# Earlier weight loads, another order in the opening, moved steps in the middle and later square roots in a fused attention and MLP kernel

## The chip, the cores and the metric

The kernel runs on one core of one Trainium2 chip. Times are device microseconds of one execution. A kernel was run once, with a profile, and where a few per cent matter in several timed rounds as well, beside runs of the kernel before on the same chip. All times compared below are of runs in the fast state. "Span" is the profiled execution from the first to the last instruction; it is some 1.7 us shorter than the time.

## The reference, cut to what matters

```python
def _attn_ref(q, k, v, lam):          # 4 batches, 8 heads, 768 rows, head size 64
    for b in range(nb):               # blocks of rows, a state of 64 x 64 per head
        intra = einsum('bhic,bhjc->bhij', qb, kb) * Dmask    # decay inside the block
        intra = einsum('bhij,bhjd->bhid', intra, vb)
        inter = einsum('bhid,bhde->bhie', qb * lam_pow, kv_state)
        out[:, :, sl] = intra + inter
        kv_state = lam_block * kv_state + einsum('bhsd,bhse->bhde', kb * rev_pow, vb)

def _moe_ref(x, g_ln, w_ch1, w_ch2):  # x: 4 x 768 x 512 out of the attention
    mu, var = mean(x), mean((x - mu) ** 2)
    xn = (x - mu) / sqrt(var + 1e-06) * g_ln
    return x + maximum(xn @ w_ch1, 0.0) @ w_ch2        # 512 -> 2048 -> 512
```

## The kernel before: the parts that matter

The work is cut into 12 units of 256 rows (a "window" is a unit's keys, queries and values). A unit goes through casts, transposes, scores and masks, products with values and state, and a norm; then its 256 rows are one group of the MLP. The two MLP weights come in four pieces each, with a cast from fp32 to bf16 in the transfer, issued by GpSimd. SyncE issues nearly everything else. A piece is held back by `behind`, a tiny GpSimd copy (0.19 us in the traces) that reads something and so waits for its landing: 7.24 us for the first piece in the kernel before.

```python
def load_w1(c):
    nc.gpsimd.dma_start(w1[c], moe_w_ch1[...])            # 512 KB in SBUF
def load_window(u, after_pool=False, parts=1):            # keys, queries, values of unit u
    got = {name: inp.tile([128, H, 2 * D], F32, tag=name + "in", ...) for name in "kqv"}
    if after_pool:
        nc.gpsimd.memset(got["k"][:, 0, 0:1], 0.0)        # the load waits for GpSimd's place
    ...  nc.sync.dma_start(got[name][:, hs, :], source(...))
def behind(tile_ap):
    seen_p = wk.tile([128, 1], F32, tag="seen_p", name="seen_p")
    nc.gpsimd.tensor_copy(seen_p, tile_ap)

# constants: allocated one after another, ahead of all the working buffers
lam_v = const.tile([128, H, 2], F32)
lam_c = const.tile([128, H], F32)
lam_s = const.tile([128, NP], F32)

# opening ...
open_window(0); load_window(1)
in_k(0, nc.vector, HA)                    # cast of the first half of the keys
transpose_pe(0, 0, (0, 1))
nc.scalar.activation(lam_c, lnlam, ACT.Exp, scale=float(C))
in_q(0, nc.vector, HA)
in_k(0, nc.gpsimd, HB)                    # second half of the keys
load_w1(0)                                # first weight piece, behind that cast
...
norm(0, 0, early=True)
behind(w1[0][:, 0, 0:1])                  # ... the next waits for the first
load_w1(1); in_q(1, nc.gpsimd); load_w1(2); load_w1(3); in_v(1, nc.gpsimd); load_w2(0)
behind(w1[2][:, 0, 0:1])
load_window(2, after_pool=True)
# ...
def p4(u):                                # at the end of a unit's norm
    to_xT(u, 0); to_xT(u, 1)              # transposed input of the MLP, by DMA from unit 2 on
    rstd_of(u)                            # ScalarE: square root of the variance
# ... and a plan: after MLP step n of TensorE, these attention steps
add(29, (s4, 3), (p4, 3), (transpose_dma, 4))
add(41, (s1, 4))
```

## Time and profile before

230.24 us, median of 3 runs (229.79 to 230.64); the span of the profiled run is 228.9 us at a granted TensorE clock of 1.000.

| engine | busy us | share of the span |
|---|---|---|
| TensorE matmuls | 204.7 | 89% |
| TensorE weight loads (beside the matmuls) | 139.4 | 61% |
| VectorE | 101.4 | 44% |
| ScalarE | 84.9 | 37% |
| GpSimd | 73.4 | 32% |

The table of stages of the kernel before shows where TensorE loses time after its first 15 us. Each row is a stretch in us from the span's start, its length, then busy us and instructions of each engine; the last two numbers are the mean busy share of the DMA engines and GB/s.

```profile
core 0: us, PE busy (x) PEld busy (x) DVE busy (x) ACT busy (x) POOL busy (x), PEclk, DMA share, GB/s
15.00:20.00 5.00, 2.80 (x30) 2.48 (x31) 1.78 (x4) 1.62 (x3) 1.82 (x3) 1.00 0.57 130
20.00:60.00 40.00, 35.18 (x538) 24.00 (x536) 17.55 (x37) 18.30 (x32) 20.83 (x27) 1.00 1.12 218
60.00:120.00 60.00, 56.82 (x986) 38.27 (x984) 30.45 (x63) 20.29 (x37) 27.46 (x32) 1.00 1.11 235
120.00:210.00 90.00, 89.27 (x1243) 59.13 (x1241) 40.57 (x87) 33.26 (x63) 17.45 (x20) 1.00 0.61 106
```

From 20 to 120 us TensorE loses 8.0 us of 100 while the DMA share is above 1 (it sums the times of packets, so a share above 1 means that some packets overlap on an engine). From 120 us on it loses 0.73 of 90, and the DMA share is 0.61. One more row of the page will be needed: what SyncE's queue moved in the whole run (packets, MB, the time of its packets as a share of 16 engines' span).

```profile
q1 hardware_dynamic: 71008, 32.65, 68.7%
```

The busy time in that row is 0.687 x 228.9 = 157.3 us of all 16 engines. I call it the queue's engine time below.

### The profile page before, as it was taken

The page shows a single profiled execution, that of the slowest core. Times are in us where ns is not written, and L with a number is a line of the kernel's source. Part 1 is how long each engine was busy: PE and PEld are TensorE (multiplying, and loading weights), DVE is VectorE, ACT ScalarE, POOL GpSimd, SP SyncE. Part 2 cuts the span into 40 slices and gives each one's busy share as a digit, 9 for nine tenths or more (in the row PEclk, how much of TensorE's full clock was granted, in tenths as well). Part 3 has the DMA queues.
Part 4 walks back from the last instruction along what each step waited for, and adds up shares of the span by engine and source line. Part 5 has one row for each costly group of instructions (what it writes and reads, how often), then busy time and mean ns, then how long its engine had stood idle before and what let it go on. Part 6 is the DMA issues. An engine that isn't in the chain of part 4 may idle for free.

```text
span 228.9 us, 6911 instructions
## 1 busy us (share of the span) xinstructions
PE 204.7 (89%) x3056; PEld 139.4 (61%) x3056; DVE 101.4 (44%) x216; ACT 84.9 (37%) x154; POOL 73.4 (32%) x93
## 2 busy tenths in 40 slices
PE   0647697989999999698999999999999999999992
PEld 0537586644575675285486485585684784765862
DVE  2761552428256155833554535437338237152011
ACT  4625557511153243035135145154252351350610
POOL 3608415707745064668028045063010010000000
PEclk9999999999999999999999999999999999999999
DMA  5996999999999999999999699695193212311303
GB/s 140 284 250 101 191 247 218 144 281 273 190 297 267 160 259 262 159 262 239 183 273 177 126 218 175 142 216 72 42 141 74 51 47 46 95 26 23 93 3 92
DMA packets 75566, 37.42 MB, mean 163 GB/s; under 512 B 31248, under 2 KB 72464, under 8 KB 75536
## 3 DMA queue, kind: packets, MB, share of 16 engines
q1 hardware_dynamic: 71008, 32.65, 68.7%
q0 software_dynamic: 4224, 4.19, 11.8%
q8 instruction: 24, 0.39, 0.7%
q10 hardware_dynamic: 304, 0.14, 0.2%
q14 instruction: 6, 0.05, 0.1%
HBM read 27.53 MB, written 6.29 MB: 148 GB/s over the span
## 4 chain that ended last, share of the span: by engine, by line
PE 52%; DMA 24%; POOL 8%; issue 6%; DVE 5%; ACT 2%; SPq 1%; DVEq 0%; POOLq 0%
PE pm L360 24%; PE pm L398 22%; DMA w<-in_moe_w_ch_dram 7%; DMA qin<-in_q_dram 6%; DMA kin<-in_k_dram 6%; POOL kq L171 3%; DMA xT<-xc 2%; DMA kqT<-kq 2%; DVE stats L310 2%; POOL kq L163 2%; POOL vb L176 2%; PE po L273 2%; PE pm2h L389 2%; DVE xc L312 1%; PE pk L232 1%
## 5 line engine op out<-in xcount | busy, mean ns | idle before, releaser
L360 PE MATMUL pm<-xT,w 128*128 128x256 bf16 x736 | 87.3, 273 | 3.4 <-DMA xT<-xc 1.3
L363 ACT ACTIVATE hT<-pm 128x512 bf16<-128x512 f32 x92 | 54.6, 596 | 91.7 <-PE pm L360 91.6
L398 PE MATMUL pm<-w,hT 128*128 128x512 bf16 x368 | 83.0, 379 | 0.4
L360 PEld LDWEIGHTS <-w 128*128 128x128 bf16 x736 | 69.8, 98 | 15.7 <-issue 3.0
L398 PEld LDWEIGHTS <-hT 128*128 128x128 bf16 x368 | 34.9, 98 | 41.6 <-ACT hT L363 2.6
L238 POOL TENSOR_TENSOR Sn<-Stmp,lam_s 128x256 bf16<-128x256 f32 x16 | 9.8, 613 | 77.2 <-DVE Stmp L242 77.2
L218 DVE TENSOR_TENSOR mA<-sc,keep 128x512 bf16<-128x512 f32 x44 | 28.6, 682 | 12.7 <-PE sc L208 12.6
L414 DVE SCALAR_TENSOR_TENSOR o<-pm,rstd,x 128x512 f32<-128x512 f32 x23 | 17.1, 745 | 35.4 <-PE pm L398 35.2
L310 DVE BATCH_NORM_STATS2 stats<-x 128x6 f32<-128x512 f32 x20 | 13.8, 689 | 28.2 <-ACT x L308 28.2
L171 POOL TENSOR_TENSOR kq<-qin,lam_q 128x512 bf16<-128x512 f32 x22 | 22.6, 1048 | 10.4 <-DMA qin<-in_q_dram 10.2
L176 POOL TENSOR_TENSOR vb<-vin,lam_v 128x1024 bf16<-128x1024 f32 (+1 forms) x13 | 23.0, 1774 | 2.7 <-DMA vin<-in_v_dram 2.6
L312 DVE SCALAR_TENSOR_TENSOR xc<-po,mv,g_row 128x512 bf16<-128x512 f32 x24 | 18.0, 751 | 2.0
L242 DVE TENSOR_TENSOR Stmp<-pk,Sn 128x256 f32<-128x256 f32 x16 | 6.8, 422 | 18.9 <-PE pk L232 18.2
L308 ACT COPY x<-po 128x512 f32<-128x512 f32 x20 | 10.9, 590 | 8.8 <-PE po L273 4.5
L185 PE MATMUL tp<-ident,kq 128*128 128x128 bf16 x48 | 5.3, 261 | 8.1 <-DVE kq L163 5.5
L273 PE MATMUL po<-vb,mA 64*64 64x64 bf16 x768 | 10.4, 199 | 1.2 <-DVE Sn L238 0.5
L163 POOL CAST kq<-kin 128x512 bf16<-128x512 f32 (+1 forms) x18 | 10.1, 588 | 4.4 <-DMA kin<-in_k_dram 4.4
L208 PE MATMUL sc<-kqT 64*64 64x128 bf16 x352 | 9.9, 223 | 1.6 <-DVE mA L218 0.8
L337 ACT ACTIVATE std<-mv,eps_t 128x2 f32<-128x2 f32 x12 | 3.6, 301 | 20.0 <-DVE mv L311 20.0
L273 PEld LDWEIGHTS <-mA 64*64 64x64 bf16 x768 | 9.2, 109 | 2.7 <-issue 2.1
L185 PEld LDWEIGHTS <-kq 128*128 128x128 bf16 x48 | 3.8, 117 | 9.4 <-DVE kq L163 5.5
L208 PEld LDWEIGHTS <-kqT 64*64 64x64 bf16 x384 | 7.3, 111 | 3.6 <-issue 3.3
(57 smaller groups left out, 95.3 us busy)
## 6 DMA issues: line engine op xcount, KB each, us to landing
kin<-in_k_dram SPq DMA_DIRECT2D x11, 512.0 KB, 5.6
qin<-in_q_dram SPq DMA_DIRECT2D x11, 512.0 KB, 6.3
vin<-in_v_dram SPq DMA_DIRECT2D x11, 512.0 KB, 7.1
out_dram<-o SPq DMA_DIRECT2D x22, 256.0 KB, 4.8
w<-in_moe_w_ch_dram POOLq DMA_DIRECT2D x8, 512.0 KB, 7.6
kin<-in_k_dram SPq DMA_DIRECT2D x2, 256.0 KB, 4.7
qin<-in_q_dram SPq DMA_DIRECT2D x2, 256.0 KB, 5.1
vin<-in_v_dram SPq DMA_DIRECT2D x2, 256.0 KB, 5.5
```

Source lines behind the costliest of these rows:

```text
L163: (eng.copy if eng is nc.scalar else eng.tensor_copy)(dst[:, :, :, j], src[:, :, :, j])
L171: eng.tensor_tensor(dst[:, :, :, j], src[:, :, :, j], lq[:, :, :, j:j + 1].to_broadcast([128, n, 2, D]), op=ALU.mult)
L176: eng.tensor_tensor(st[u]["vb"][:, hs], qkv_in[u]["v"][:, hs], lam_v[:, hs, :, None].to_broadcast([128, n, 2, D]), op=ALU.mult)
L208: nc.tensor.matmul(sc[e][half[ab], i, jk, :], lhsT=kT[half[e], 2 * hf + i, jk, half[ab]], rhs=qT[half[e], 2 * hf + i, :, half[ab]], start= ...
L218: nc.vector.tensor_tensor(s[f"mA{hf}"][:, e], s[f"sc{hf}"][e], kp[:, None, :, :].to_broadcast([128, 2, 2, 128]), op=ALU.mult)
L273: nc.tensor.matmul(s["po"][ab][half[jq], 2 * p + e, :], lhsT=s[f"mA{p // 2}"][half[ab], e, p % 2, j, half[jq]], rhs=s["vb"][half[ab], 2 * ...
L310: nc.vector.bn_stats(stats, po if early else x)
L312: nc.vector.scalar_tensor_tensor(xc, in0=po, scalar=mv[:, 0:1], in1=g_row, op0=ALU.subtract, op1=ALU.mult)
L360: nc.tensor.matmul(pm[:, b, :], lhsT=w1[n // W2K][:, kk, (n % W2K) * 128:(n % W2K + 1) * 128], rhs=xT_of[g][:, kk, 0:N], start=(b == 0 and ...
L363: nc.scalar.activation(hT[:, u * NB:(u + 1) * NB, 0:N], pm, ACT.Relu)
L398: nc.tensor.matmul(acc[i], lhsT=hT[:, kk, i * 128:(i + 1) * 128], rhs=w2[kk // W2K][:, kk % W2K, :], start=(kk == 0), stop=(kk == KB - 1))
L414: nc.vector.scalar_tensor_tensor(o[:, ab], in0=a, scalar=rstd[:, ab:ab + 1], in1=x[:, ab], op0=ALU.mult, op1=ALU.add)
```

## The change

Its intent: fetch the MLP weights earlier, so that TensorE doesn't wait for them and the loads behind them move up too; shorten the opening; move steps of units 3 to 7 so that masks and transposed inputs are ready in time; and keep the square roots out of the way of the Relus. The diff, cut to its core:

```diff
-    lam_c = const.tile([128, H], F32)
 ...
-    nc.scalar.activation(lam_c, lnlam, ACT.Exp, scale=float(C))
+    for e in range(2):
+        nc.scalar.activation(lam_s[half[e]], ln_p[half[e], :, e], ACT.Exp, scale=float(C))
     in_q(0, nc.vector, HA)
+    behind(qkv_in[0]["k"][:, 0, 0, 0:1])
+    load_w1(0)
     in_k(0, nc.gpsimd, HB)
-    load_w1(0)
+    transpose_pe(0, 1, (0, 1))
     transpose_pe(0, 0, (2, 3), nc.vector)
-    for e in range(2):
-        nc.vector.tensor_copy(lam_s[half[e]], lam_cp[half[e], :, e])
-    transpose_pe(0, 1, (0, 1))
 ...
-    behind(w1[0][:, 0, 0:1])
+    behind(qkv_in[1]["k"][:, 0, 0, 0:1])
     load_w1(1)
+    load_w1(2)
     in_q(1, nc.gpsimd)
-    load_w1(2)
     load_w1(3)
+    load_w2(0)
     in_v(1, nc.gpsimd)
-    load_w2(0)
 ...                       # w2 pieces 2 and 3 likewise ahead of in_q(2) and in_v(2)
 def p4(u):
-        rstd_of(u)        # now a step of its own: add(at + 9, (rstd_of, j - 1)) and so on
 ...                       # middle of the plan
-    add(7, (p0, 3, nc.vector))                     # to step 11
-    add(26, (load_one, 6, "k"))                    # to 30
-    add(29, (s4, 3), (p4, 3), (transpose_dma, 4))  # s4, p4 to 30; the transposes to 25
-    add(41, (s1, 4))                               # to 39
-    add(42, (p0, 6))                               # to 40
-    add(43, (s2, 4), (load_one, 7, "q"))           # to 41
-    add(45, (s3, 4), (load_one, 7, "v"))           # to 43
-    add(46, (s4, 4), (p4, 4))                      # to 45
-    add(52, (s2, 5))                               # to 53
```

More of the change, by code (lines that the diff above doesn't have):

```diff
@@ L457 @@
         nc.scalar.activation(lam_v[:, :, j], lnlam, ACT.Exp, scale=e_v[:, j:j + 1])
-    nc.scalar.activation(lam_c, lnlam, ACT.Exp, scale=float(C))
+    ln_p = lnlam.rearrange("p (a two) -> p a two", two=2)
+    for e in range(2):
+        nc.scalar.activation(lam_s[half[e]], ln_p[half[e], :, e], ACT.Exp, scale=float(C))
     nc.vector.tensor_tensor(lam_q[:, :, 1], lam_q[:, :, 0], lam_b, op=ALU.mult)
     in_q(0, nc.vector, HA)
+    behind(qkv_in[0]["k"][:, 0, 0, 0:1])
+    load_w1(0)
     in_k(0, nc.gpsimd, HB)
-    load_w1(0)
     in_q(0, nc.vector, HB)
+    transpose_pe(0, 1, (0, 1))
     transpose_pe(0, 0, (2, 3), nc.vector)
-    lam_cp = lam_c.rearrange("p (a two) -> p a two", two=2)
-    for e in range(2):
-        nc.vector.tensor_copy(lam_s[half[e]], lam_cp[half[e], :, e])
-    transpose_pe(0, 1, (0, 1))
     transpose_pe(0, 1, (2, 3))
@@ L542 @@
     load_w2(1)
+    load_w2(2)
     in_q(2, nc.gpsimd)
-    load_w2(2)
+    load_w2(3)
     in_v(2, nc.gpsimd)
-    load_w2(3)
     load_window(3, after_pool=True)
@@ L633 @@
     add(6, (s2, 2))
-    add(7, (p0, 3, nc.vector))
     add(9, (s3, 2))
-    add(11, (s4, 2), (p4, 2), (transpose_dma, 3))
+    add(11, (s4, 2), (p4, 2), (p0, 3, nc.vector), (transpose_dma, 3))
     for n, name in zip((12, 14, 16), "kqv"):
         add(n, (load_one, 5, name))
+    add(15, (rstd_of, 2))
     add(17, (p0, 4))
@@ L641 @@
     add(26, (s2, 3))
-    add(26, (load_one, 6, "k"))
+    add(25, (transpose_dma, 4))
     add(28, (s3, 3), (p0, 5))
-    add(29, (s4, 3), (p4, 3), (transpose_dma, 4))
+    add(30, (s4, 3), (p4, 3), (load_one, 6, "k"))
     add(31, (load_one, 6, "q"))
+    add(34, (rstd_of, 3))
     add(32, (load_one, 6, "v"))
@@ L648 @@
     add(38, (load_one, 7, "k"))
-    add(41, (s1, 4))
-    add(42, (p0, 6))
-    add(43, (s2, 4), (load_one, 7, "q"))
-    add(45, (s3, 4), (load_one, 7, "v"))
-    add(46, (s4, 4), (p4, 4))
+    add(39, (s1, 4))
+    add(40, (p0, 6))
+    add(41, (s2, 4), (load_one, 7, "q"))
+    add(43, (s3, 4), (load_one, 7, "v"))
+    add(45, (s4, 4), (p4, 4))
     add(46, (transpose_dma, 6))
-    add(50, (s1, 5))
+    add(50, (s1, 5), (rstd_of, 4))
     add(51, (p0, 7))
-    add(52, (s2, 5))
+    add(53, (s2, 5))
     for n, name in zip((48, 50, 52), "kqv"):
@@ L668 @@
         add(at + 4, (s2_s4, j), (p4, j - 1))
+        add(at + 9, (rstd_of, j - 1))
         if j + 3 < NU:
@@ L673 @@
     add(154, (s4, NU - 1), (p4, NU - 1))
+    add(159, (rstd_of, NU - 1))
     for i, (f, *a) in enumerate(plan):
```

## The prediction

> **What bounds the kernel now.** I read, in this order: the page's slices, TensorE's waits, the chain of waits, GpSimd's timeline, the DMA queues in short windows, and one iteration of the steady part.
>
> Slices first: TensorE's row, the DMA row, and the chain's summary by engine.
>
> ```profile
> PE   0647697989999999698999999999999999999992
> DMA  5996999999999999999999699695193212311303
> ...
> PE 52%; DMA 24%; POOL 8%; issue 6%; DVE 5%; ACT 2%; SPq 1%; DVEq 0%; POOLq 0%
> ```
>
> A slice is 5.7 us. TensorE is full from about 40 us on; its holes are in the first seven slices and in slice 17. The whole span is 228.9 us with 204.7 us of matmul, so 24.2 us are idle: 16.2 of them before 60 us (43.8 busy of 60 in the table of stages), the rest in the tail and in short waits. The DMA engines are full over the first 22 slices except the fourth (17 to 23 us). The first quarter is thus a race of loads; the rest is matmul. Where TensorE waited:
>
> ```profile
> PE tp L185 <- DVE kq L163: 5.5, 1, 5.5
> PE xt L331 <- DVE xc L312: 2.0, 2, 1.8
> PE pm1t L372 <- DMA w<-in_moe_w_ch_dram: 2.0, 1, 2.0
> PE tp L185 <- POOL kq L171: 1.4, 2, 0.8
> ...
> PE pm L360 <- DMA xT<-xc: 1.3, 1, 1.3
> PE pm L360 <- issue: 1.3, 2, 1.0
> PE po L286 <- DVE seen L297: 1.1, 1, 1.1
> PE sc L208 <- DVE mA L218: 0.8, 1, 0.8
> ```
>
> Columns: total us, times, longest. The 5.5 is the first load and nothing in the change touches it. The others are small, and each has a date: the weight wait ends at 18.15 us, the `kq L171` waits at 38.2 and 39.2, the `seen` wait at 51.8, `mA` at 94.8, `xT` at 97.5, "issue" at 107.3 and 123.6. The chain of waits (start, length, what) says what stands behind the early ones:
>
> ```profile
> 7.65 10.46 DMA w<-in_moe_w_ch_dram
> ...
> 21.12 5.86 DMA w<-in_moe_w_ch_dram
> ...
> 27.69 9.36 DMA qin<-in_q_dram
> ...
> 42.74 8.16 DMA kin<-in_k_dram
> 50.90 0.02 issue
> 50.93 0.76 DVE kq L163 x2
> ```
>
> The first weight piece is asked for at 7.65 and lands at 18.1. The third is asked for at 21.1, lands at 27.0, and only then are the loads of window 2 issued, whose queries release GpSimd at 37.1. GpSimd then frees the issue of window 3 at 42.6, whose keys land at 50.9 and hold VectorE, and through it `seen` and TensorE. It is one serial ladder of landings. GpSimd's own timeline shows its first rung held back:
>
> ```profile
> 7.65 0.94 POOL L89 DMA_DIRECT2D w<-in_moe_w_ch_dram  x1
> 8.85 2.07 POOL L176 TENSOR_TENSOR vb<-vin,lam_v 128x512 bf16<-128x512 f32 x2 [0.27 <-DMA vin<-in_v_dram]
> 18.16 0.19 POOL L450 CAST seen_p<-w 128x1 f32<-128x1 bf16 x1 [7.24 <-DMA w<-in_moe_w_ch_dram]
> 18.28 0.81 POOL L89 DMA_DIRECT2D w<-in_moe_w_ch_dram  x1
> ```
>
> GpSimd stands 7.24 us idle because the second piece waits for the landing of the first, and meanwhile the DMA engines run dry: share 0.64 in 16 to 18 us and 0.20 in 18 to 20, against 1.0 to 1.25 around it. That is about 2.5 us of transfer time lost; another 1.5 us is lost at 38 to 42 (shares 0.81 and 0.70).
>
> [...] after the issue at 7.65 the GpSimd queue moved no packet before 12 us, while SyncE's queue worked off what it had (718 packets in 8 to 10 us, 1194 in 10 to 12); from 12 to 14 the two moved 216 and 562. The piece issued at 33.5 also moved nothing before 36. So I reckon with something near to first come, first served. [...] the first weight piece's last packets moved in the 16 to 18 us window and its landing was at 18.1. [...] Here the three loads take 1.28 us each; moving square roots among Relus adds none (12 roots, no further load in the trace), and the moved Exp still stands before the first root.
>
> One iteration of the steady part, all engines:
>
> ```profile
> 156.09 7.35 PE L398 MATMUL pm<-w,hT 128*128 128x512 bf16 x32
> ...
> 158.55 0.29 ACT L337 ACTIVATE std<-mv,eps_t 128x2 f32<-128x2 f32 x1 [2.15 <-DVE mv L311]
> ...
> 158.76 0.58 ACT L363 ACTIVATE hT<-pm 128x512 bf16<-128x512 f32 x1
> ...
> 159.38 3.57 PEld L398 LDWEIGHTS <-hT 128*128 128x128 bf16 x18 [0.60 <-ACT hT L363]
> ```
>
> The root waits 2.15 us for the variance; the last Relu of the group, whose input was ready near 156.2, stands behind it; after 14 of 32 matmuls the weight load has no `hT`. The 32 matmuls take 7.35 us there and 7.07 at 107.66, 124.04 and 203.84: 0.28 us lost, not the 0.60 of the weight load row. I find it at 139.9, 156.1, 172.3 and 188.4.
>
> **The change part by part.** (a) Opening. One 0.20 us Exp becomes two on half the partitions, and two VectorE copies (1.08 us, 8.87 to 9.95) go; the mask starts at 10.04, right behind them, so it may start 0.1 to 0.3 earlier. Query transposes ahead of the second key half fill the 1.23 us hole before 7.42, but the last transpose still waits for queries at 8.6. Taken: 0.2 us.
>
> (b) First weight piece. It goes behind the landing of the first key half (issue 0.81 + 4.3 = 5.1) instead of behind GpSimd's cast: issue near 5.35, 2.3 us earlier. The 0.94 us of issue ends at 6.3, before the second key half lands (6.96), so the cast loses nothing. First come, first served puts the piece behind `g_row` (issued 5.12) and before the keys of window 1 (5.94): data from about 9, done about 13.2 (4.5 us, as it had beside another queue), landing about 15. The first layer's first tile then waits for its transposed input alone, at 16.3 instead of 18.15. Gain 1.85, less where the queries of window 1 come late: 1.8 us.
>
> (c) Next pieces. Keys of window 1 land not at 12.9 but about 15, pushed by the piece ahead. Pieces 2 and 3 are issued there, about 15.1 and 15.9 instead of 18.3 and 21.1, and their data follow the backlog at 17 without the dry stretch. At 2.6 to 3.2 us a piece (528 packets at the 205 per us of 24 to 27 us, or 163 of 22 to 24) they land near 21 and 24; TensorE needs piece 2 at 22. Window 2 is then issued at 24 instead of 27.3. Its queries land near 33.5 instead of 37.05, and TensorE wants them at 35.7: the two `kq L171` waits (0.58 + 0.78) go. Taken: 1.3 us. Window 3 is issued near 38 instead of 42.6, its keys land near 45, and its cast moves behind the norm of unit 2: the `seen` wait goes, 1.1 us.
>
> (d) Middle. Unit 4 moves up by one or two steps, one second score step moves from 52 to 53, unit 3's last step back by one. A step of four matmuls is 0.87 us. They aim at `mA` (0.8) and `xT` (1.3). But removing the first lets TensorE arrive at the second 0.8 us sooner while the transposed input lands at best 0.87 sooner, and the DMA share there is 1.6 to 2.1. So I take 0.9 of the 2.1, nothing of the issue waits.
>
> (e) Roots placed later: 4 x 0.28 = 1.1 us.
>
> Sum: 0.2 + 1.8 + 1.3 + 1.1 + 0.9 + 1.1 = 6.4 us. 230.24 - 6.4 = 223.8 us, 2.8% less.
>
> **Rivals.** First: the early weights only take bandwidth from queries and values of windows 0 and 1. [...] the values of unit 0 land late; they have little slack (GpSimd waited 0.27 us for them) and the queries of window 1 come 1 to 2 us later. For it: DMA share at 1.1 from 4 to 8 us. Against it: the FIFO-like packet counts. It would take back 1 to 2 us: 225 to 226. Second: the ladder is shorter, but a full TensorE only arrives early at a DMA-bound middle: share above 1.0 in nearly every stage from 20 to 120 us, so that waits for `xT` at the start of groups 2, 3 or 4 grow. For it: the transposed input of unit 3 landed at about 76.9 for a start at 77.15, and its step is now 0.87 later. Against it: the DMA work itself moves up by some 4 us, and unit 4's key transposes now leave earlier. If (d) gains nothing and 1.5 us come back: 226. Third: all holes of the middle close, the issue waits too (they come beside a full DMA): (d) gives 3 instead of 0.9, 221.7.
>
> **Range and chances.** The early gains (4.2) and the roots (1.1) each rest on a wait that is seen; I trust their sum to about 1.5 us. The middle can be -1.5 to +3. 8 times in 10: 221.3 to 227.0. Faster by over 2% means below 225.6, which is within the first rivals' reach: 0.77 faster, 0.22 within 2%, 0.01 slower.
>
> **What would show it.** Right: the first weight issue near 5.4 and its landing near 15; no weight wait before the first tile at 16.3; no dry DMA slice at 17 to 23 us; window 2 issued near 24; `kq L171` and `seen` gone from TensorE's waits; every steady group of 32 matmuls at 7.07 us and the row of weight loads waiting for `hT` empty. Wrong: values of unit 0 later than 9.6 us or queries of window 1 later than 18 [...]; a new `xT`, `kqT` or weight wait on TensorE at the start of a group; a 7.35 us group that stays, which would mean that the Relu is late for another cause than the root.

## The result, and the profile after

The kernel after takes 221.2 us (median of 4 fast runs, 220.95 to 221.83); the kernel before took 230.44 us in the same rounds (229.79 to 230.99). Ratios here and below are the mean time of one kernel's fast runs over that of the other's of the same rounds, so not quite the ratio of the medians: 0.9604, with a 95% interval of 0.9571 to 0.9637. All runs of both were fast. The span went from 228.9 to 219.5 us.

Slices of TensorE and of the DMA engines, and the chain's summary by engine, of the kernel after (a slice is 5.5 us):

```profile
PE   0859699999999999899999999999999999999992
DMA  4999999999998999899995895992492302310303
...
PE 85%; DVE 6%; DMA 4%; ACT 3%; issue 1%; POOL 0%; DVEq 0%
```

The dry DMA slice at 17 to 23 us is gone, and the hole of TensorE in slice 17 went from 6 to 8 tenths busy. The chain that ends last is 85% matmul, where it was 52%, with 24% DMA. TensorE's waits (total us, times, longest):

```profile
PE tp L184 <- POOL seen_p L449: 5.4, 1, 5.4
PE xt L330 <- DVE xc L311: 2.0, 2, 1.8
PE pm L359 <- DVE mA L217: 0.8, 1, 0.8
PE tp L184 <- DVE kq L170: 0.6, 1, 0.6
PE pm L359 <- DMA xT<-xc: 0.6, 1, 0.6
```

The first row is the old wait for the first load under a new releaser. The waits for weights, for `kq L171`, for `seen`, and both issue waits are gone; that for `xT` went from 1.3 to 0.6. GpSimd's timeline (start, length, what, idle before) has the new ladder:

```profile
5.32 0.94 POOL L89 DMA_DIRECT2D w<-in_moe_w_ch_dram  x1
...
14.79 0.19 POOL L449 COPY seen_p<-kin 128x1 f32<-128x1 f32 x1 [4.54 <-DMA kin<-in_k_dram]
14.92 1.56 POOL L89 DMA_DIRECT2D w<-in_moe_w_ch_dram  x2
...
23.24 0.19 POOL L449 CAST seen_p<-w 128x1 f32<-128x1 bf16 x1 [1.01 <-DMA w<-in_moe_w_ch_dram]
```

The first piece is issued at 5.32 us instead of 7.65, the next two at 14.92 instead of 18.28 and 21.12, and the landing that frees the loads of window 2 is seen at 23.24 instead of 27.04. The stages of the kernel after, in the columns of the table before:

```profile
15.00:20.00 5.00, 4.65 (x60) 4.38 (x59) 1.63 (x3) 3.88 (x7) 4.72 (x6) 1.00 1.13 233
20.00:60.00 40.00, 37.56 (x591) 25.64 (x589) 20.27 (x41) 17.60 (x32) 20.13 (x23) 1.00 1.13 253
60.00:120.00 60.00, 59.16 (x981) 39.16 (x980) 32.88 (x68) 22.37 (x41) 30.55 (x34) 1.00 1.01 222
120.00:210.00 90.00, 90.00 (x1237) 61.92 (x1236) 37.03 (x79) 34.49 (x63) 12.42 (x14) 1.00 0.49 99
```

In 60 to 120 us TensorE gained 2.34 us, at a DMA share that went down, from 1.11 to 1.01. That is more than the moved steps were to give, and I had expected no fall of that share. The steady part, where the 7.35 us group was:

```profile
147.49 7.07 PE L397 MATMUL pm<-w,hT 128*128 128x512 bf16 x32
...
147.69 0.61 ACT L362 ACTIVATE hT<-pm 128x512 bf16<-128x512 f32 x1
...
150.37 0.29 ACT L336 ACTIVATE std<-mv,eps_t 128x2 f32<-128x2 f32 x1 [2.08 <-DVE mv L310]
```

The Relu comes first, the root after it, and the group takes 7.07 us. Last, SyncE's queue:

```profile
q1 hardware_dynamic: 71008, 32.65, 64.8%
```

The same packets and bytes, but 0.648 x 219.5 = 142.2 us of engine time instead of 157.3. Nothing in the visible change makes a transfer cheaper.

The start of the same work in both traces gives the lead of the kernel after as it grows. The terms in the last column are the steps of the prediction.

| start of | before | after | lead | new lead | predicted |
|---|---|---|---|---|---|
| first scores | 9.36 | 8.69 | 0.67 | 0.67 | (a) 0.2 |
| first weight tile | 18.15 | 15.81 | 2.34 | 1.67 | (b) 1.8 |
| work after unit 2's queries | 39.63 | 35.79 | 3.84 | 1.50 | (c) 1.3 |
| work after the `seen` wait | 52.06 | 47.06 | 5.00 | 1.16 | (c) 1.1 |
| group 4, second layer | 107.66 | 99.45 | 8.21 | 3.21 | (d) 0.9 |
| last part of the last layer | 221.18 | 211.74 | 9.44 | 1.23 | (e) 1.1 |

So five terms were sized to about half a microsecond and one, the middle, was 2.3 us short. One trace of each kernel stands behind these leads.

### The profile page after: what moved, and what is told of

It is laid out like the page before. It is cut to its first block, busy times and chain, and to the rows that moved or that the text cites. A ratio compares the mean times of both kernels' runs of the same rounds, so it can differ in the third digit from the quotient of the medians.

```text
span 219.5 us, 6919 instructions
## 1 busy us (share of the span) xinstructions
PE 203.4 (93%) x3056; PEld 139.5 (64%) x3056; DVE 101.4 (46%) x214; ACT 85.3 (39%) x155; POOL 74.3 (34%) x94
## 4 chain that ended last, share of the span: by engine, by line
PE 85%; DVE 6%; DMA 4%; ACT 3%; issue 1%; POOL 0%; DVEq 0%
PE pm L397 35%; PE pm L359 35%; PE po L272 3%; PE sc L207 3%; DVE mA L217 2%; DMA xT<-xc 2%; PE po L285 2%; PE pk L231 2%; PE pm1t L371 2%; PE pm2h L388 2%; DMA lam_b<-in_lam_dram 2%; PE tp L184 2%; DVE xc L311 1%; DVE stats L309 1%; ACT kqT L185 1%
## 5 line engine op out<-in xcount | busy, mean ns | idle before, releaser
L397 PE MATMUL pm<-w,hT 128*128 128x512 bf16 x368 | 82.1, 379 | 0.0
L359 PEld LDWEIGHTS <-w 128*128 128x128 bf16 x736 | 69.6, 98 | 13.3 <-DMA xT<-xc 1.4
L397 PEld LDWEIGHTS <-hT 128*128 128x128 bf16 x368 | 35.4, 98 | 40.2
L309 DVE BATCH_NORM_STATS2 stats<-x 128x6 f32<-128x512 f32 x20 | 13.8, 690 | 30.4 <-ACT x L307 30.4
L162 POOL CAST kq<-kin 128x512 bf16<-128x512 f32 (+1 forms) x18 | 10.7, 621 | 0.4 <-DMA kin<-in_k_dram 0.4
L336 ACT ACTIVATE std<-mv,eps_t 128x2 f32<-128x2 f32 x12 | 3.6, 301 | 15.1 <-DVE mv L310 15.1
```

The lines of the kernel that those rows point to most:

```text
L309: nc.vector.bn_stats(stats, po if early else x)
L359: nc.tensor.matmul(pm[:, b, :], lhsT=w1[n // W2K][:, kk, (n % W2K) * 128:(n % W2K + 1) * 128], rhs=xT_of[g][:, kk, 0:N], start=(b == 0 and ...
L397: nc.tensor.matmul(acc[i], lhsT=hT[:, kk, i * 128:(i + 1) * 128], rhs=w2[kk // W2K][:, kk % W2K, :], start=(kk == 0), stop=(kk == KB - 1))
```

## The experiments

My first theory was that the parts are worth what the prediction gave them, with the middle gaining more because the moved steps hit more waits than I had counted. The rival: the middle's waits close by themselves once everything arrives earlier. Four kernels did parts of the change on the kernel before. They share their runs of the kernel before (median 231.1 us). All kernels below gave correct results.

### Early: the weight pieces and the opening, nothing else

```diff
+    (the change's hunks for lam_c, the opening and the weight pieces)
     (the square roots and the plan of the middle as before)
```

> The kernel before with only the early part of the change: the opening (two Exps instead of Exp and two copies, query transposes first) and the order of the weight pieces; middle steps and square roots as before. My theory: the early holes go one by one, lead at the start of group 2's first layer 5.0 to 5.2 us (opening 0.66, first tile 1.7, queries of window 2 1.4, seen wait 1.2), and nothing more is gained or lost after it but the issue waits: 230.4 - 5.0 = 225.4 us. Rival (a full TensorE only arrives early at a DMA-bound middle): part is given back between groups 3 and 5, lead at the end 3 us or less, 227.5 us. Whether the issue waits near groups 4 and 5 stay is open: if they belong to the order of the middle steps they stay at 1.3 us, if to the timing of the loads they change.

Measured: 224.89 us (4 runs), ratio 0.9717 (0.9674 to 0.9761). The time is 0.5 us under the one expected, but the kernel before was slower in these rounds than the 230.4 us that I had reckoned from: the gain is 6.2 us by the medians, not 5.0. And the issue waits were gone and `xT` stood at 1.0 us, without one moved step; and its queue's engine time was 0.650 x 223.3 = 145.1 us. The middle has a part that is not in its plan.

### Middle: only the moved steps

```diff
-    add(41, (s1, 4))
+    add(39, (s1, 4))
     (and the other moved steps, as in the change)
```

> The kernel before with only the moved steps of units 3 to 7 (the square roots stay where they were, in the same step as the transposes). My theory: the mA wait (0.8 in the row, 1.0 by the clock) and most of the xT wait (1.3 to 0.6) go, and the seen wait (1.1) too because the cast of unit 3's keys stands behind the norm of unit 2: 230.4 - 2.9 = 227.5 us; with the issue waits gone too 226.2 us. Rival (these steps only pay once the early loads are ahead): under 1 us, 229.5 us.

Measured: 232.44 us (20 runs), ratio 1.0057 (1.0033 to 1.0082): no gain but a small loss. My expectation (a gain of 2.9 us) missed by some 4 us. The waits of TensorE, and its timeline at the start of group 4:

```profile
PE pm L360 <- DMA xT<-xc: 4.6, 2, 3.4
```
```profile
98.20 4.46 PE L360 MATMUL pm<-xT,w 128*128 128x256 bf16 x24 [3.41 <-DMA xT<-xc]
```

The `seen` wait, the second-score `mA` wait and the issue waits did go, and one wait for the transposed input took more than all of it back: group 4 starts at 98.20 us instead of 97.51. The DMA share was 1.41 from 94 to 98 us: the two transposes issued from 90.1 to 92.8 us took 5.3 and 7.6 us to land, beside other work of the DMA engines, as the second rival of the prediction had it. What made them land in time in the kernel after was still open.

The timeline shows a second loss that I first passed over. The 24 matmuls behind the wait took 4.46 us; in the kernel before they took 2.79. The stages (columns as above, the granted clock stands before the DMA share) show a lower clock after the 3.41 us of idle time:

```profile
98.00:100.00 2.00, 1.80 (x10) 1.35 (x11) 0.00 (x0) 0.04 (x1) 1.16 (x1) 0.62 1.09 209
100.00:103.00 3.00, 3.00 (x60) 2.19 (x62) 0.00 (x0) 1.45 (x3) 0.00 (x0) 0.68 0.98 273
```

In the kernel before it was 1.00 in both stretches. So this profile loses 0.7 us to the later start and 1.7 us to the clock, and gets 1.0 us back from the issue wait that is gone: the second layer of group 4 starts at 109.02 us instead of 107.66. Whether every one of the 20 runs lost clock there isn't known.

### Roots: only the later square roots

```diff
 def p4(u):
-        rstd_of(u)
+    add(15, (rstd_of, 2)); add(34, (rstd_of, 3)); add(50, (rstd_of, 4))
+    add(at + 9, (rstd_of, j - 1)); add(159, (rstd_of, NU - 1))
```

> The kernel before with only the square roots placed later. Theory: the four groups of 32 second-layer matmuls at 7.35 us become 7.07, nothing else moves: 230.4 - 1.1 = 229.3 us, issue waits stay at 1.3. Rival (the Relu is late for another cause): 230.4 us and the 7.35 groups stay.

Measured: 229.72 us (12 runs), ratio 0.9931 (0.9899 to 0.9962), span 1.0 us shorter. All groups of 32 matmuls of the second layer took 7.07 us; the waits of the middle stayed. This term is what it was taken for.

### Opening: only the Exp and the order of transposes

```diff
-    lam_c = const.tile([128, H], F32)
-    nc.scalar.activation(lam_c, lnlam, ACT.Exp, scale=float(C))
+    (two Exps into the halves of lam_s; query transposes ahead of the second key half)
```

> The kernel before with only the opening (two Exps, no VectorE copies, query transposes first); weight pieces as before. Theory: the first masks and the first norm come 0.6 us earlier, but the first weight piece still lands at 18.1 and takes all of it back: weight wait 2.6 instead of 2.0, 230.4 us. Rival: the opening is worth its 0.6 by itself: 229.8 us.

Measured: 228.55 us (4 runs), ratio 0.9875 (0.9817 to 0.9934). That is a gain of 2.5 us by the medians, where none was expected. The weight wait was 2.6 us, as expected:

```profile
PE pm1t L371 <- DMA w<-in_moe_w_ch_dram: 2.6, 1, 2.6
```

The first weight tile starts at 18.40 us, 18.15 in the kernel before, so what the opening can have given was lost again by then. Yet the `seen` wait at 51.8 us and the issue waits at 107 and 123 us were gone, far from anything that this kernel edits. Engine time: 0.643 x 227.1 = 146.0 us. A kernel that differs in a 0.2 us Exp, two copies and the order of transposes moves the same bytes in 11 us less of engine time.

The only other thing that it does is to delete `lam_c`, a tile of 32 bytes per partition. In the program as it is built (no trace shows addresses) nearly everything allocated after it moves by 32 bytes: the load buffers `kin`, `qin` and `vin`, the casts `kq`, the transposed `kqT`, the outputs `o`. `kin` starts at byte 54048 = 211 x 256 + 32 of a partition in the kernel before, and at 54016 = 211 x 256 in the kernel after. New theory: transfers are cheaper where the buffers start at a multiple of some number of bytes; the diff's most valuable line for the middle is the deletion of a tile. The rival: the opening's earlier start shifts the phase of loads against each other, and the waits vanish by that.

### Pad: the kernel before with 32 bytes more

```diff
-    lam_c = const.tile([128, H], F32)
+    lam_w = const.tile([128, 2 * H], F32)
+    lam_c = lam_w[:, 0:H]
```

This puts the buffers at a multiple of 64 (64 past a multiple of 256). No instruction changes.

> The kernel before with 32 unused bytes per partition added to one small tile, nothing else: all tiles allocated after it move by 32 bytes, so that the buffers of keys, queries, values and of both transposes start at a multiple of 64 bytes as they do in the changed kernel (which lost a 32-byte tile); in the kernel before they start 32 bytes off. Theory (the hidden part of the change is this shift): SyncE's queue takes 145 to 147 us of 16 engines instead of 157, the issue waits go, and the time is that of the run of the opening alone, ratio 0.985 to 0.990. Rival (the opening's earlier masks and copies gave that run its gain): ratio 1.000, engine time of the queue unchanged.

Measured: 230.72 us (the 16 fast runs of 20), ratio 0.9983 (0.9958 to 1.0008). No gain: with 64 bytes as the number the theory fell. The profiled run of this kernel was a slow one (233.65 us at a clock of 0.993), so I read nothing finer from its trace.

### After_shift: the kernel after with 32 bytes more

```diff
-    lam_s = const.tile([128, NP], F32)
+    lam_w = const.tile([128, 3 * NP], F32)
+    lam_s = lam_w[:, 0:NP]
```

The whole visible change, with the buffers 32 bytes past a multiple of 256, as in the kernel before.

> The changed kernel with 32 unused bytes added, so that the buffers are 32 bytes off again as in the kernel before. Theory: engine time of SyncE's queue back to 153 to 157 us instead of 142, waits for transposed inputs [...] come back in the middle, ratio to before 0.968 to 0.975 (223 to 224.5 us instead of 221.2). Rival (alignment does nothing): ratio 0.960.

Measured: 225.69 us (4 runs), ratio 0.977 (0.9726 to 0.9815). Spare bytes in a constant cost some 4 us (1.7%). The waits and the queue's row:

```profile
PE pm L360 <- issue: 1.4, 2, 0.8
PE pm L360 <- DMA xT<-xc: 1.0, 1, 1.0
```
```profile
q1 hardware_dynamic: 71008, 32.65, 69.4%
```

The issue waits are back, and 0.694 x 223.4 = 155.0 us of engine time. The rival (phase of the opening) falls here: this kernel has the opening of the change. My number of 64 had fallen with `pad`; what fits both runs is a larger number.

### Weights: only the order of the weight pieces

```diff
+    behind(qkv_in[0]["k"][:, 0, 0, 0:1])
+    load_w1(0)
     in_k(0, nc.gpsimd, HB)
-    load_w1(0)
     (and the later pieces, as in the change; lam_c stays)
```

> The kernel before with only the order of the weight pieces and of what GpSimd does among them; opening, middle steps, roots and layout of the memory (32 bytes off) as before. By the sum of my prediction: first tile 1.8, query waits 1.3, seen wait 1.1, together 4.2 us, ratio 0.982. If gains of loads and alignment simply add (early 0.9717 less opening 0.9875): 3.6 us, ratio 0.984. Rival (without the alignment the weights only displace queries and keys): ratio 0.990 or more.

Measured: 226.86 us (4 runs) against 231.02, ratio 0.9812 (0.9758 to 0.9866). As expected. The profiled run was the slowest of the four (228.44 us), so its trace shows less than the gain. TensorE's first weight tile starts at 16.73 us; the `seen` wait is gone though the step kept its place in the plan, so it was the ladder of loads that freed it, as the prediction had argued. What stays is the middle:

```profile
PE pm L360 <- DMA xT<-xc: 1.5, 1, 1.5
PE pm L360 <- issue: 1.3, 2, 0.7
```

### Pad_middle: the middle's steps on the kernel with 32 bytes more

```diff
     (middle, with lam_c in a tile of 2 * H as in pad)
```

> The run of the middle steps alone (ratio 1.0057, its 3.4 us wait for the transposed input of unit 4 at the start of group 4) with the 32 bytes added. Theory (the middle is bound by the DMA engines and the moved steps ask for more of them earlier than they can give): with the cheaper transfers the wait shrinks to about 1 us, and the run comes out at or under that of the 32 bytes alone: ratio 0.980 to 0.988. Rival (the moved steps cost by their order, whatever the DMA does; only the earlier loads pay for them): the wait stays above 3 us, ratio 0.992 or more.

Measured: 231.63 us (20 runs), ratio 1.0025 (0.9996 to 1.0053); the `xT` wait is 4.0 us, and the granted clock behind it was 0.50 for 5.4 us (0.975 over the whole profiled run). No help from 64 bytes here either.

### Pad224 and pad96: which number of bytes

```diff
-    lam_c = const.tile([128, H], F32)
+    lam_w = const.tile([128, 64], F32)      # pad224: 224 bytes more, a multiple of 256
+    lam_w = const.tile([128, 32], F32)      # pad96:   96 bytes more, a multiple of 128
+    lam_c = lam_w[:, 0:H]
```

> The kernel before with 224 unused bytes, nothing else: the buffers of keys, queries, values and of the transposed keys and queries start at a multiple of 256 bytes, as in the changed kernel (they are at 256 x 211 and on there). The 32-byte pad put them at a multiple of 64 only and changed nothing. Theory [...]: engine time of SyncE's queue 143 to 147 us instead of 154 to 157, and the gain of the opening run is this: ratio 0.985 to 0.992. Rival (the opening's own steps, or something else in that run, make the transfers cheaper): engine time stays at 154 to 157, ratio 0.998 to 1.000.

> The same with 96 unused bytes: these buffers start at an odd multiple of 128 bytes (the transposed inputs of the MLP, by chance, at a multiple of 256). If 256 bytes are what counts: engine time 152 to 157 us, ratio 0.996 to 1.002. If 128 bytes are enough: as with 224 bytes, 143 to 147 us, ratio 0.985 to 0.992.

Measured: pad224 226.67 us (4 runs) against 230.11, ratio 0.9846 (0.9804 to 0.9889); pad96 232.12 us (6 runs), ratio 1.006 (1.0023 to 1.0098). The same instructions in the same order, and of the numbers tried only 256 bytes counts. The queue's row of pad224:

```profile
q1 hardware_dynamic: 71008, 32.65, 64.6%
```

That is 0.646 x 224.8 = 145.2 us. Pad96 has 0.653 x 230.5 = 150.5 us, a little less than the 154 to 158 of the other shifted kernels and than the 152 to 157 expected, and no gain in time from it. The clock is not the cause: by the runs whose mean granted clock was 0.998 or more, pad224 took 226.53 us (median of 3), pad96 230.48 (2), the kernel before 230.02 (9). The other four runs of pad96, at 0.993, took 232.1 to 232.4; in the profiled one the clock was 0.59 from 108 to 112 us, behind an issue wait of 2.0 us. So its loss of 0.6% is not the price of 128 bytes. Of pad224's waits in the middle little was left:

```profile
PE pm L361 <- issue: 0.3, 1, 0.3
PE pm L361 <- DMA xT<-xc: 0.2, 1, 0.2
```

### Aligned: the kernel after with every buffer of a transfer at 256 bytes

In the kernel after, `xT` and the weights still start 128 bytes past a multiple of 256 and `xc` 64. This kernel pads five small tiles so that these start at one too. It was meant to beat both kernels.

```diff
+    eps_w = const.tile([128, 32], F32); eps_t = eps_w[:, 0:1]
+    lam_w = const.tile([128, 48], F32); lam_s = lam_w[:, 0:NP]
     (and seen, mv, seen_p padded likewise)
```

> The changed kernel with every buffer that a DMA fills or reads put at a multiple of 256 bytes: also the weights (at 128 off in both kernels), the transposed inputs (128 off) and their sources (64 off). Theory: engine time of SyncE's queue 138 to 142 us instead of 142, of GpSimd's 25 to 26 instead of 27; the waits for transposed inputs at the start of groups 4 and 5 (0.6 and 0.3) shrink: ratio 0.955 to 0.960, 220 to 221 us. Rival (what is left is off the path): 0.960, 221.2 us.

Measured: 222.16 us (6 runs), ratio 0.9643 (0.96 to 0.9686), span 219.1 us, engine time 143.7 us. No gain that can be seen, and GpSimd's queue stayed as it was (26.7 us of engine time, 26.8 in the kernel after). The `xT` wait went from 0.6 to 0.2 us and the span from 219.5 to 219.1, less than the scatter of the six runs (220.83 to 223.34).

### Pad224_middle: the middle's steps where the buffers start at 256 bytes

```diff
     (middle, with lam_c in a tile of 64 as in pad224)
```

> The moved middle steps alone (ratio 1.0057 where the buffers are 32 bytes off, 3.4 us of waiting for the transposed input of unit 4) with the 224 bytes of the last but one call (0.9846 without the moved steps). Theory (the moved steps ask the DMA engines for more in less time; where the transfers are cheap they pay): the wait is under 1.5 us, no issue wait, ratio 0.976 to 0.982. Rival (they pay only with the weights and windows ahead, whatever a transfer costs): the wait stays near 3 us, ratio 0.985 to 0.992.

Measured: 226.85 us (4 runs), ratio 0.9785 (0.974 to 0.983). The wait that spoilt `middle`:

```profile
PE pm L361 <- DMA xT<-xc: 1.2, 1, 1.2
```

1.2 us instead of 4.6, and the 24 matmuls behind it take 2.79 us again, as in the kernel before, where the granted clock was 1.00. The moved steps go from a loss of 0.6% to a gain of 0.9785 / 0.9846 = 0.994, some 0.6%, though the intervals of these two overlap, so the gain is likely and not sure.

### The parts together

| kernel | buffers past a multiple of 256 bytes | engine time us | ratio |
|---|---|---|---|
| before | 32 | 157.3 | 1 |
| weights | 32 | 154.2 | 0.981 |
| roots | 32 | 157.5 | 0.993 |
| middle | 32 | 156.0 | 1.006 |
| all visible parts (after_shift) | 32 | 155.0 | 0.977 |
| pad_middle | 64 | 154.7 | 1.003 |
| pad96 | 128 | 150.5 | 1.006 |
| opening | 0 | 146.0 | 0.988 |
| pad224 | 0 | 145.2 | 0.985 |
| pad224_middle | 0 | 146.2 | 0.979 |
| early | 0 | 145.1 | 0.972 |
| after | 0 | 142.2 | 0.960 |
| aligned (`xT`, `xc` and weights at 0 too) | 0 | 143.7 | 0.964 |

The visible parts without the shift give 0.977, the shift alone 0.9846; their product is 0.962, beside 0.9604 measured. So the two add up within the intervals, and together they are the whole result. In us of the 231 before: 5.3 for the visible parts and 3.6 for the shift. Among the visible parts, weights and roots alone make 0.9812 x 0.9931 = 0.974 of the 0.977; the opening's steps add nothing that can be seen (opening 0.9875 beside pad224 0.9846), and with the buffers 32 bytes off the times are too wide (some 0.5% each way) to tell what the middle's steps add.

Which transfers became cheaper shows in two ways. One is the shortest landing of each kind, from its issue, over a whole run. For `kqT` the profile's line (the first of the three numbers), before and in pad224:

```profile
DMA to landing us min/median/max: 3.3/4.9/7.7
DMA to landing us min/median/max: 2.7/5.1/7.0
```


| us | before | after_shift | pad96 | opening | pad224 | after |
|---|---|---|---|---|---|---|
| `kqT` transposes | 3.3 | 3.2 | 3.2 | 2.7 | 2.7 | 2.8 |
| keys | 4.3 | 4.5 | 4.5 | 4.5 | 4.2 | 4.1 |

The transposes of keys and queries split cleanly by alignment: every one of the kernels run has 3.2 to 3.3 us off 256 bytes and 2.7 to 2.8 at it. The transposes into `xT` show no such difference: 2.3 to 2.4 us in the eight kernels read for it (before, roots, after_shift, pad96, opening, pad224, after, aligned). The shortest landings of keys overlap.

The other is the record of every packet that the traces keep (the views don't print it). The packets of SyncE's queue sort by size: 512 bytes are loads of keys, queries and values, 256 bytes are transposes, 2048 bytes are stores of the result. Their times, summed, in us of 16 engines:

| packets | before | after_shift | pad96 | opening | pad224 | after |
|---|---|---|---|---|---|---|
| 36864 of 512 bytes, loads | 70.4 | 71.3 | 70.6 | 65.3 | 65.8 | 64.5 |
| 28672 of 256 bytes, transposes | 58.1 | 55.6 | 52.9 | 51.7 | 51.9 | 52.1 |
| 3072 of 2048 bytes, stores | 23.0 | 23.7 | 23.3 | 23.9 | 23.1 | 22.2 |

Over all 14 kernels the loads split cleanly: 69.6 to 71.8 us off 256 bytes, 64.3 to 65.8 at it. Most of their packets take 27 ns; off 256 bytes 29 to 42% took more than 30 ns, at it under 3%. The transposes take 52.9 to 58.3 and 51.7 to 55.0, which overlap; the stores show no difference. So of the 12 us between before and pad224 the loads are 4.6 and the transposes 6.2.

## Why the prediction was right or wrong, point by point

The call, faster by more than 2%, was right, and the time came out 0.1 us under the low edge of the range. It came there with one term that the prediction did not have: some 3.6 us of the gain are the shift, which no step of it names, so there is luck in it: without the shift the ratio is 0.977, and its interval reaches over 0.98. One reading was loose without harm: the first DMA slice is half empty too, not only the fourth.

- (a) Opening, 0.2 us: 0.67 by these two traces. With the old opening the first scores start at 9.36 to 9.74 us in nine traces, whatever the alignment, and the kernel before has the earliest of them. With the new opening they start at 8.69 to 8.96 at 256 bytes and at 9.34 in the one trace off it (after_shift). So by itself the opening gave 0 to 0.4 us by that one trace, and more only together with the shift.
- (b) First weight piece, 1.8 us: 1.67 by the clock, and 16.46 us for the first weight tile in after_shift, 1.69 earlier. Issue at 5.32 (predicted 5.35), landing at 13.8 (predicted 15), the tile then waiting only 0.3 us for its transposed input. Its packets ended at 13.4 (predicted 13.2) and it landed 0.4 us later (0.3 in the kernel before: 17.8 and 18.1). The prediction had allowed 1.8 us for that; this was the author's estimate, and windows of 2 us could not check it. Packet counts agree with something near to first come, first served: the piece moved nothing in 6 to 8 us and 130 packets in 8 to 10. From 8 us on both queues moved packets (130 of GpSimd's and 246 of SyncE's to 10 us, 292 and 237 to 12), so a late start of the piece's own packets is not excluded. The first rival did not show: the values of unit 0 did not come late.
- (c) Queries and `seen`, 2.4 us: 2.66 measured. Keys of window 1 at 14.79 (predicted 15), pieces 2 and 3 issued from 14.92 (15.1), window 2 after 23.2 (24). The kernel with the weight pieces alone gained 231.02 - 226.86 = 4.2 us (1.2 either way); (b) and (c) had summed to 4.2.
- (d) Middle: this is the step that failed. "So I take 0.9 of the 2.1, nothing of the issue waits"; it was 3.2. The reasoning around it was right for the program that I thought I was looking at: with the buffers 32 bytes off, the whole change (after_shift) gains 1.24 us in this stretch and keeps the issue waits, at 1.4 us, and the moved steps alone lose 0.6%, to the second rival's wait for `xT` (up to 3.4 us at once) and the low clock behind it (0.62 to 0.68 in that trace). What I did not see is that deleting `lam_c` moves the buffers to a multiple of 256 bytes and takes 8% off the queue's engine time (157.3 to 145.2 us in pad224), where this stretch has a DMA share above 1 (1.11 from 60 to 120 us). The third rival's outcome came (holes closed, issue waits too, 3 instead of 0.9), for another cause than the one it had.
- (e) Square roots, 1.1 us: 1.23 by the clock, 1.0 in the span of the kernel that has them alone. All the 7.35 us groups became 7.07. ScalarE has three ACT_TABLE_LOADs of 1.28 us in the traces of both kernels, so the moved roots and Exps added none.

Without the hidden shift, the predicted 6.4 us would have been 5.3. The trace of after_shift, read at the six starts of the table above, has new leads of 0.02, 1.67, 0.63, 1.16, 1.24 and 0.81 us for 0.2, 1.8, 1.3, 1.1, 0.9 and 1.1 predicted (one trace each; the first scores alone scatter by 0.4 us). So the queries' part of (c) leaned on the shift as well. The kernel after has 0.65 more at the first scores, 0.87 more at the queries, 1.97 more in the middle and 0.42 more at the end: the shift added these.

Open: how much of (b) and (c) is the first piece's earlier issue and how much the later pieces' waiting for keys rather than for weights (not run apart).

On what the issue waits are, the kept traces say this. Each run has a DMA queue named `instruction` with 24 packets of 16384 bytes, and TensorE's 6112 instructions in the trace of the kernel before are just under 24 times 256. All 13 issue waits of 0.2 us or more behind the first load, in all 14 traces, stand at an instruction whose number (by start) is 186 to 193 past a multiple of 256, and end 1.3 to 1.6 us after a packet of that queue ends. From these numbers I take them for waits for the next block of instructions; no trace names what ends them. What makes the block late is open. The waits at the end of a first layer sum to 1.2 to 1.4 us in before, roots, weights and after_shift (32 bytes off) and 2.0 in pad96; the longest are 1.0 us, at 106.3 us of the kernel before, and the 2.0 of pad96. They are 0.3 us in pad and absent in middle and pad_middle, though these are off 256 bytes as well, and at most 0.3 us in every kernel at 256. In the kernel before, the DMA share beside its two was 1.86 (106.0 to 107.3 us) and 1.23 (123.0 to 123.6); that crowded DMA engines make the block late was not shown.

## What to carry to other kernels

Read a diff for what it does to addresses as well as to instructions: here a 32-byte constant that went moved nearly every buffer allocated after it, and with a DMA share of 1.11 to 1.12 from 20 to 120 us such a move alone was 1.5% (pad224, 0.9846). When a kernel's part gains something far from its edit, compare the queue's engine time (share times span) at equal packets and bytes before looking for a cause in the order of work. And test a move of steps under the load it will run in: the same moves lost 0.6% where the queue's engine time was 156.0 us (middle) and seem to gain as much where it was 146.2 (pad224_middle).
